# A delta-rule attention with two MLPs: stage b ahead of the merge in odd steps, one negation of 96 partitions, and GpSimd's zeros in place of two masks

## The chip, the cores and the metric

One core of a Trainium2 chip runs the whole program. The metric is device microseconds of one execution; the median of three runs of the kernel before is 896.2 us.

## The reference

The inputs are q, k, v of 4 batches x 8 heads x 768 tokens x 48 features and a step size beta. The attention is a recurrence over tokens, and its output feeds two dense blocks:

```python
for t in range(S):
    kt, vt, bt = (k_n[:, :, t], v[:, :, t], beta[:, :, t, None])
    y[:, :, t] = np.einsum('bhd,bhde->bhe', q[:, :, t], state)
    v_old = np.einsum('bhde,bhd->bhe', state, kt)
    state = state + bt[:, :, :, None] * np.einsum('bhd,bhe->bhde', kt, vt - v_old)
...
X = fft(fft(x, axis=1), axis=2); u = x + real(X)
y = u + relu(layernorm(u) @ w_ch1) @ w_ch2                      # 384 -> 1536 -> 384
h = relu(y @ w_in); u, v = halves(h)                            # 512 each
out = (u * (w_spatial @ layernorm(v) + b_spatial)) @ w_out
```

## The kernel before

**Chunks.** The recurrence is cut into 48 chunks of 64 tokens (12 of each batch, the batches interleaved), numbered bc. One chunk holds all 8 heads of its batch as 4 pairs, so a tile has 128 partitions: two heads of 64 tokens. Inside a chunk the recurrence is the inverse of a triangular 64x64 matrix. It is built from two 32x32 inverses and one corner block between them.

**The solve.** Six blocks of 8 chunks are inverted on VectorE (DVE). `prep` gathers the two 32x32 diagonal blocks of every head into `Cc`, masks them for blocks 1 and 2 only (L255), and transposes them into `Ts`. `root` reads their diagonal (`sq`, L140) and has ScalarE (ACT) take a square root (L141). `solve` runs the elimination column by column (L271 to L314) and transposes the inverse to `Tc` (L324). The solve of block j is spread over eight steps of the loop, and the `prep` and `root` of block j+1 stand at its end. GpSimd (POOL) only sets the diagonal to one (L274).

**The loop.** Step t, from -3 to 47, issues for different chunks:

- values (L400, ACT, four scalings of the loaded k and v of chunk t+2 by the norms);
- stage d of chunk t (L436 and L438 on TensorE, PE; then ACT copies the new state `Sb`, L449, and the output `x`, L453);
- stage c of chunk t+1 (L423 on PE, then `cw` on DVE, L424; stage d of that chunk multiplies by `cw`);
- stage a of chunk t+20 while there are such chunks (L217 on PE, then L223 on DVE);
- in odd steps `merge` of a pair of chunks, in even steps `diag` (L363, ACT);
- stage b of chunk t+2 (L407 on PE, then two ACT copies into `WU`, L412).

**The merge** makes the corner blocks of two chunks. PE interleaves two kinds of 32x32 matmuls into the one bank Z: `z0` (L375) for the pair that comes next, `z1` (L377) for the pair whose `z0` an earlier merge made. ACT then negates `z0` into `ZS` in two instructions of 32 partitions (L380), and copies `z1` into the inverse `TT` in two (L383). `z1` of the next merge reads `ZS`. Stage b of the pair reads `TT`, and first does so in the next, even step. At the first pair of a block an additional merge with `z0` alone stands between stage d and stage c (t % 8 == 5); at the last pair of a block the merge has `z1` alone.

**Order.** The engines execute what the code issues in the order of issue: `chain` ties every instruction to the one ahead of it on its engine. So the order in the code is the order in each engine's queue. From t = 37 on values and `diag` run on DVE, and pieces of the Fourier transform (L616 to L660) and of the weight conversion (L690 to L703) fill the gaps. The MLPs follow after about 300 us.

```python
qs = [slice(32 * u, 32 * u + 32) for u in range(4)]
lo, up = qs[::2], qs[1::2]
```

Of the kernel before, what the change touches and what calls it, by code (L numbers as in the profile page):

```python
# [7 lines left out]
F32 = mybir.dt.float32  # L8
# [12 lines left out]
C = 64  # L21
NC = S // C
HP = H // 2
NBC = B * NC
# [41 lines left out]
class Kernel:  # L66
# [51 lines left out]
    def attention(self, cp, pg, pe, p, x, filler, after_solves):  # L118
        nc, a, load = self.nc, self.a, self.load
        bt = cp.tile([128, NBC * HP], F32, name="bt")  # L120


        mk = cp.tile([128, 4 * C + 66], F32, name="mk")
        ZS = [cp.tile([128, 8, 64], F32, name=f"ZS{i}") for i in range(2)]
# [8 lines left out]
        gas, Tts, st, kqs, qts, preps, seen_a = {}, {}, {}, {}, {}, {}, [0]  # L133


        def root(blk):

            Tf, T = preps[blk]
            sq, n0 = (pe.tile([128, 32], F32, name=n, bufs=2) for n in ("sq", "n0"))
            nc.vector.tensor_copy(out=sq, in_=Tf[:, 0:1024:33])  # L140
            nc.scalar.sqrt(n0, sq)  # L141
            preps[blk] = Tf, T, sq, n0

# [100 lines left out]
        def prep(blk):  # L244


            Cc = pe.tile([128, 1024], F32, name="Cc").rearrange("p (g c) -> p g c", g=32)
            for h4 in range(2):
# [4 lines left out]
                yield 750  # L253
            if blk in (1, 2):
                nc.vector.tensor_mul(Cc, Cc, mk[:, 4 * C + 2 : 4 * C + 34].unsqueeze(1).to_broadcast([128, 32, 32]))  # L255
                yield 1200

            Tf = pe.tile([128, 1056], F32, name="Ts", bufs=CF["mb"])
            T = Tf[:, :1024].rearrange("p (i j) -> p i j", i=32)
            nc.vector.transpose(out=T, in_=Cc.rearrange("p g c -> p c g"))  # L260
            preps[blk] = Tf, T
            yield 2000
# [91 lines left out]
        lo, up = qs[::2], qs[1::2]  # L354
# [10 lines left out]
        def merge(g8, first, second):  # L365
# [4 lines left out]
            tt = TT[(g8 - 1) % NTT]  # L370
            for g in range(8):
                for h in range(2):
                    if first:
                        ga = gas[g8 * 2 + g // 4][:, g % 4]
                        nc.tensor.matmul(z0[up[h], g], lhsT=ga[up[h], C : C + 32], rhs=T0[up[h], o0 + g], start=True, stop=True)  # L375
                    if second:
                        nc.tensor.matmul(z1[lo[h], g], lhsT=T1[lo[h], o1 + g], rhs=ZS[(g8 - 1) % 2][lo[h], g], start=True, stop=True)  # L377
            if first:
                for h in range(2):
                    nc.scalar.mul(ZS[g8 % 2][lo[h], :, 32:], z0[up[h]], -1.0)  # L380
            if second:
                for h in range(2):
                    nc.scalar.copy(out=tt[lo[h], :, 64 * h : 64 * h + 64], in_=z1[lo[h]])  # L383

# [90 lines left out]
        for t in TT:  # L475
            nc.gpsimd.memset(t, 0.0)
        zz = self.bank("pz", [128, 512])
        for t in ZS:
            nc.scalar.copy(out=t[:, :, :32], in_=mk[:, 4 * C + 34 :].unsqueeze(1).to_broadcast([128, 8, 32]))
        for t in WU + Sb:  # L480
# [31 lines left out]
        T0 = -3  # L512
        for t in range(T0, NBC):
# [31 lines left out]
            if t < T0 + CF["kq"]:  # L545
                load_kq(HEAD + t - T0)
            if t % 2:
                g = (t + 3) // 2
                if g < NBC // 2:
                    merge(g + 1, (g + 1) % 4 > 0, True)  # L550
            elif t % 8 != 4 and t + 4 < NBC:
                diag((t + 4) // 2)
            if (t + 4) % 8 > 1 and t + 4 < NBC:
                load_kv(t + 4)
            if light(t):
# [4 lines left out]
                for _ in range(CF["cvt"][t - (NBC - 11)]):  # L560
                    next(tail, None)
            if 0 <= t + 2 < NBC:
                stage_b(t + 2)
# [544 lines left out]
def layout(q, k, v, beta, moe_w_ch1, moe_w_ch2, moe2_w_in, moe2_w_spatial, moe2_b_spatial, moe2_w_out):  # L1108
# [36 lines left out]
    j, s2 = KEY[s], np.where(s < 32, (s <= i) & (i < 32), (i < 32) | (s <= i))  # L1145
    o["mk"] = np.concatenate([j + i < C, s2, j < i, s2, s >= 32, s < 32, s % 32 <= i[:, :32], s % 32 == i[:, :32]], 1).astype(f)
    o["idn"] = np.eye(128, dtype=f)
# [69 lines left out]
```

## Time and profile before

| What | us |
| --- | --- |
| Median of 3 runs (lowest 895.42, highest 898.05) | 896.2 |
| The profiled execution | 895.05 |
| Its span in the profile, first to last instruction | 892.9 |
| PE busy over the span | 849.1 |
| DVE busy | 578.0 |
| ACT busy | 404.9 |
| POOL busy | 71.1 |
| Start to the first merge / loop with merges / MLPs | 0 to 41 / 41 to 275 / 300 to 893 |

An engine's busy time is the sum of its instructions' durations; neighbours on one engine overlap a little, so a sum can come close to the stretch without leaving a real gap. PE being busy 95% of the span says little of the loop: there its busy share changes from stretch to stretch, and what counts is which engine another waits for.

### The profile page before, as it was taken

To read this page: it belongs to the slowest core of one execution; us is meant where nothing else is said; L and a number is where in the kernel's file an instruction comes from. 1 tells how busy PE (TensorE), PEld (TensorE's weight loads), DVE (VectorE), ACT (ScalarE), POOL (GpSimd) and SP (SyncE) were. 2 spreads that over 40 slices of the span, in tenths; PEclk is the share of its full clock that TensorE was granted. 3 is DMA by queue.
4 is the path that set the end of the run, shared out by engine and by line. 5 is a ranking of instruction groups with operands and counts; after the bars stand their busy time and mean duration, and the time that the engine had idled before them with its cause. 6 is when DMAs were issued, how large, how long until landed. Compare 5 with 4: busy or idle time off the path is not lost.

```text
span 892.9 us, 18553 instructions
## 1 busy us (share of the span) xinstructions
PE 849.1 (95%) x7219; PEld 817.5 (92%) x7219; DVE 578.0 (65%) x1786; ACT 404.9 (45%) x1014; POOL 71.1 (8%) x75
## 2 busy tenths in 40 slices
PE   7779989998998899999999999999999999999998
PEld 7678989888898798999999999999889899899898
DVE  5999998988766898785574793431475562451622
ACT  2589888789875544321212352221262241341411
POOL 2000000000000000000000000000033232222221
PEclk8969999999999899999999999999999999999999
DMA  8264666633461710001022311101132210000001
GB/s 217 75 179 119 172 170 162 164 82 81 121 172 46 268 69 1 1 1 27 1 63 80 124 28 27 37 18 32 45 92 68 75 28 28 27 1 28 28 1 54
DMA packets 57674, 67.24 MB, mean 75 GB/s; under 512 B 31825, under 2 KB 48946, under 8 KB 57586
## 3 DMA queue, kind: packets, MB, share of 16 engines
q1 hardware_dynamic: 57586, 66.05, 26.0%
q8 instruction: 57, 0.93, 0.5%
q14 instruction: 31, 0.25, 0.1%
HBM read 53.64 MB, written 4.72 MB: 65 GB/s over the span
## 4 chain that ended last, share of the span: by engine, by line
PE 77%; DVE 12%; ACT 8%; issue 2%; DMA 1%; POOL 0%; ACTq 0%; DVEq 0%; POOLq 0%
PE bankX L801 15%; PE bankY L817 14%; PE bankX L940 11%; PE bankY L960 6%; PE bankX L926 5%; PE bankX L901 5%; PE bankY L423 4%; PE bankY L436 3%; PE bankY L438 2%; PE bankY L407 2%; PE bankX L217 2%; PE bankZ L377 2%; ACT WU L412 2%; ACT TT L383 2%; PE bankX L622 2%
## 5 line engine op out<-in xcount | busy, mean ns | idle before, releaser
L801 PE MATMUL bankX<-uh,w 128*128 128x384 f32 x504 | 136.8, 338 | 2.4 <-DVE ul L729 2.4
L817 PE MATMUL bankY<-w,hh 128*128 128x384 f32 x504 | 117.4, 339 | 1.1 <-DVE w L703 1.1
L808 ACT ACTIVATE hh<-bankX 128x384 fp32r<-128x384 f32 x84 | 41.2, 491 | 152.0 <-PE bankX L801 149.4
L809 DVE SCALAR_TENSOR_TENSOR hl<-bankX,hh 128x384 fp32r<-128x384 f32 x84 | 46.5, 554 | 97.5 <-ACT hh L808 97.4
L940 PE MATMUL bankX<-ws,vh 128*128 128x384 f32 x384 | 97.6, 336 | 0.0
L801 PEld LDWEIGHTS bankX<-uh,w 128*128 128x128 f32 x504 | 91.9, 188 | 3.1 <-DVE ul L729 2.9
L817 PEld LDWEIGHTS bankY<-w,hh 128*128 128x128 f32 x504 | 90.1, 188 | 2.2 <-DVE w L703 1.7
L801 PE MATMUL bankX<-ul,w 128*128 128x384 f32 x252 | 84.9, 337 | 0.0
L918 POOL TENSOR_TENSOR vl<-v,vh 128x512 fp32r<-128x512 f32 x24 | 31.8, 1335 | 519.8 <-DMA x<-un 442.7
L436 PE MATMUL bankY<-WU,gak 128*112 128x96 f32 (+1 forms) x384 | 69.0, 268 | 3.5 <-ACT x L453 3.2
L817 PE MATMUL bankY<-w,hl 128*128 128x384 f32 x252 | 72.2, 338 | 0.0
L940 PEld LDWEIGHTS bankX<-ws,vh 128*128 128x128 f32 x384 | 69.4, 188 | 0.0
L948 DVE TENSOR_TENSOR g<-bankX,bsb 128x384 f32<-128x384 f32 x32 | 17.7, 556 | 77.8 <-PE bankX L940 73.6
L438 PE MATMUL bankY<-Sb,cw 112*112 112x96 f32 (+1 forms) x352 | 63.9, 264 | 1.0 <-ACT w L702 0.7
L940 PE MATMUL bankX<-ws,vl 128*128 128x384 f32 x192 | 63.7, 336 | 0.0
L310 DVE TENSOR_TENSOR Ts<-Ts,tm 128x110 f32<-128x110 f32 (+26 forms) x264 | 60.4, 271 | 0.8
L305 DVE TENSOR_TENSOR tm<-Ts 128x110 f32<-128x110 f32 (+26 forms) x264 | 60.1, 270 | 0.4
L407 PE MATMUL bankY<-gak,TT 128*128 128x96 f32 x384 | 54.8, 288 | 5.1 <-issue 2.7
L436 PEld LDWEIGHTS bankY<-WU,gak 128*112 128x112 f32 (+1 forms) x384 | 52.7, 179 | 5.0 <-ACT x L453 4.8
L407 PEld LDWEIGHTS bankY<-gak,TT 128*128 128x128 f32 x384 | 49.1, 200 | 7.7 <-issue 3.0
L423 PE MATMUL bankY<-gak,WU 128*112 128x112 f32 x352 | 45.6, 274 | 8.0 <-ACT WU L412 8.0
L926 PE MATMUL bankX<-xh,s 128*128 128x384 f32 x192 | 50.3, 338 | 1.6 <-ACT v L910 1.6
(180 smaller groups left out, 1834.6 us busy)
## 6 DMA issues: line engine op xcount, KB each, us to landing
kq<-in_kq_dram SPq DMA_DIRECT2D x24, 448.0 KB, 4.3
qt<-in_qt_dram SPq DMA_DIRECT2D x48, 196.0 KB, 4.0
gak<-in_kv_dram SPq DMA_DIRECT2D x48, 192.0 KB, 4.0
w<-in_w_dram SPq DMA_DIRECT2D x24, 384.0 KB, 6.7
x<-un SPq DMA_DIRECT2D x128, 36.0 KB, 1.9
out_dram<-ot SPq DMA_DIRECT2D x24, 192.0 KB, 2.0
kq<-in_kc_dram SPq DMA_DIRECT2D x8, 448.0 KB, 11.5
s<-in_wi_dram SPq DMA_DIRECT2D x6, 512.0 KB, 4.8
```

What stands on the lines that cost most here:

```text
L305: nc.vector.tensor_tensor(out=tm, in0=T[:, r, k : k + 1].to_broadcast(sh), in1=T[:, k : k + 1, :k].to_broadcast(sh), op=MUL)
L310: nc.vector.tensor_add(o, o, tm)
L407: nc.tensor.matmul(pb[:, hp].rearrange("p t d -> p (t d)"), lhsT=tt[:, o + hp], rhs=kv[:, hp], start=True, stop=True)
L423: nc.tensor.matmul(pc[:, hp], lhsT=w[:, hp], rhs=gas[bc][:, hp, : C + D], start=True, stop=True)
L436: nc.tensor.matmul(pd[:m, hp], lhsT=ak[:, hp, :m], rhs=u[:, hp], start=True, stop=(c == 0))
L438: nc.tensor.matmul(pd[:m, hp], lhsT=cw[:, hp, :m], rhs=sb[:, hp], start=False, stop=True)
L801: nc.tensor.matmul(ph, lhsT=w1[f][i][:, c * 128 : c * 128 + 128], rhs=cur[k][:, c], start=(c + j == 0), stop=(c == 2 and j == 2))
L809: nc.vector.scalar_tensor_tensor(out=hl, in0=ph, scalar=0.0, in1=hh.bitcast(F32), op0=MAX, op1=SUB)
L817: nc.tensor.matmul(acc[t], lhsT=hx[i][:, t * 128 : t * 128 + 128], rhs=w2[e][k], start=(e == 0 and j == 0), stop=(e == 11 and j == 2),)
L926: nc.tensor.matmul(pu, lhsT=wi[2 * c][i][:, f * 128 : f * 128 + 128], rhs=xT[hf][k][:, c], start=(c + j == 0), stop=(c == 2 and j == 2),)
L940: nc.tensor.matmul(pv, lhsT=vn[i][:, s, f * 128 : f * 128 + 128], rhs=ws[2 * s + hf][k], start=(s + j == 0), stop=(s == 5 and j == 2),)
L960: nc.tensor.matmul(po, lhsT=gt[i][:, f, t * 128 : t * 128 + 128], rhs=wo[f][k], start=(f + j == 0), stop=(f == 3 and j == 2),)
```

## The change

Three edits, and what goes with them:

- **Order in odd steps.** Up to t = 43 stage b of chunk t+2 is issued ahead of the merge, no longer behind it. Even steps and the last two odd ones keep their order.
- **One negation.** `z0` is now written into the partitions 0 to 31 and 64 to 95 of bank Z, `z1` into 32 to 63 and 96 to 127 (they change places). One ACT instruction over the partitions 0 to 95 negates `z0`; it also negates the 32 partitions in between, which nobody reads. VectorE zeroes the bank once at the start. The copies into `TT` now go from one group of partitions to another.
- **Zeros in place of masks.** For blocks 1 and 2 the mask multiplication in `prep` is gone (and the step of 1200 that it counted for in the spreading of the solve). In its place `root` has POOL write zeros over the triangle of `Ts`, in five memsets of 256, 128, 64, 32 and 16 elements a partition. `Ts` is 16 columns wider, the table of masks 32 columns narrower.

```diff
-            Tf, T = preps[blk]
+            Tf, T, _ = preps[blk]
             sq, n0 = (pe.tile([128, 32], F32, name=n, bufs=2) for n in ("sq", "n0"))
             nc.vector.tensor_copy(out=sq, in_=Tf[:, 0:1024:33])
             nc.scalar.sqrt(n0, sq)
+            if blk in (1, 2):
+
+                for n in (16, 8, 4, 2, 1):
+                    t = preps[blk][2][:, n : n + 1056].rearrange("p (m q) -> p m q", q=66 * n)[:, :, : 32 * n]
+                    nc.gpsimd.memset(t.rearrange("p m (r w) -> p m r w", w=32)[:, :, :, :n], 0.0)
...
-            if blk in (1, 2):
-                nc.vector.tensor_mul(Cc, Cc, mk[:, 4 * C + 2 : 4 * C + 34].unsqueeze(1).to_broadcast([128, 32, 32]))
-                yield 1200
-
-            Tf = pe.tile([128, 1056], F32, name="Ts", bufs=CF["mb"])
+            Tw = pe.tile([128, 1072], F32, name="Ts", bufs=CF["mb"])
+            Tf = Tw[:, :1056]
...
-                        nc.tensor.matmul(z0[up[h], g], lhsT=ga[up[h], C : C + 32], rhs=T0[up[h], o0 + g], start=True, stop=True)
+                        nc.tensor.matmul(z0[lo[h], g], lhsT=ga[up[h], C : C + 32], rhs=T0[up[h], o0 + g], start=True, stop=True)
...
-                        nc.tensor.matmul(z1[lo[h], g], lhsT=T1[lo[h], o1 + g], rhs=ZS[(g8 - 1) % 2][lo[h], g], start=True, stop=True)
+                        nc.tensor.matmul(z1[up[h], g], lhsT=T1[lo[h], o1 + g], rhs=ZS[(g8 - 1) % 2][lo[h], g], start=True, stop=True)
             if first:
-                for h in range(2):
-                    nc.scalar.mul(ZS[g8 % 2][lo[h], :, 32:], z0[up[h]], -1.0)
+                nc.scalar.mul(ZS[g8 % 2][:96, :, 32:], z0[:96], -1.0)
             if second:
                 for h in range(2):
-                    nc.scalar.copy(out=tt[lo[h], :, 64 * h : 64 * h + 64], in_=z1[lo[h]])
+                    nc.scalar.copy(out=tt[lo[h], :, 64 * h : 64 * h + 64], in_=z1[up[h]])
...
         zz = self.bank("pz", [128, 512])
+        nc.vector.memset(zz, 0.0)
...
-            if t % 2:
+            odd = t % 2 and (t + 3) // 2 < NBC // 2
+            if odd and 0 <= t + 2:
+                stage_b(t + 2)
+            if odd:
                 g = (t + 3) // 2
-                if g < NBC // 2:
-                    merge(g + 1, (g + 1) % 4 > 0, True)
-            elif t % 8 != 4 and t + 4 < NBC:
+                merge(g + 1, (g + 1) % 4 > 0, True)
+            if t % 2 == 0 and t % 8 != 4 and t + 4 < NBC:
                 diag((t + 4) // 2)
...
-            if 0 <= t + 2 < NBC:
+            if not odd and 0 <= t + 2 < NBC:
                 stage_b(t + 2)
```

How the edits move instructions shows best in three places of the queues. The first is PE's queue in the odd step t = 19, at the last pair of a block, where the merge has only its 16 matmuls of `z1` (L377). Before, in the order stage c, stage a, merge, stage b, and stage d of the next step:

```order
L423 MATMUL bankY<-gak,WU_87 112x112 x4
L217 MATMUL bankX<-kq 128x128 x4
L377 MATMUL bankZ<-ZS_81,Tc 32x64 x16
L407 MATMUL bankY<-gak,TT_85 128x96 x4
L436 MATMUL bankY<-WU_87,gak 112x96
L438 MATMUL bankY<-Sb_91,cw 112x96
```

And now, with the changed kernel's line numbers (stage b is L408, the merge L379, stage d L437 and L439):

```order
L424 MATMUL bankY<-gak,WU_87 112x112 x4
L222 MATMUL bankX<-kq 128x128 x4
L408 MATMUL bankY<-gak,TT_85 128x96 x4
L379 MATMUL bankZ<-ZS_81,Tc 32x64 x16
L437 MATMUL bankY<-WU_87,gak 112x96
L439 MATMUL bankY<-Sb_91,cw 112x96
```

Stage b and the merge have changed places; all else stands where it stood.

The second place is ACT's queue in the odd step t = 13, the first pair of a block with its two merges. Before, with both negations in two halves (L380), the copies of the inverse (L363, L383), the copies of stage b (L412), and the scalings of the next step (L400):

```order
L380 ACTIVATE ZS_80<-bankZ 32x8x32 x2
L363 COPY TT_85<-Tc 32x8x32 x2
L380 ACTIVATE ZS_81<-bankZ 32x8x32 x2
L383 COPY TT_85<-bankZ 32x8x64 x2
L412 COPY WU_88<-bankY 64x4x2x48 x2
L400 ACTIVATE gak<-gak,n_all 128x48 x4
```

And now (negation L381, copies L365 and L384, copies of stage b L413, scalings L401):

```order
L381 ACTIVATE ZS_80<-bankZ 96x8x32
L365 COPY TT_85<-Tc 32x8x32 x2
L413 COPY WU_88<-bankY 64x4x2x48 x2
L381 ACTIVATE ZS_81<-bankZ 96x8x32
L384 COPY TT_85<-bankZ 32x8x64 x2
L401 ACTIVATE gak<-gak,n_all 128x48 x4
```

The two `WU` copies now come ahead of the odd merge's negation and `TT` copies, and each negation is one instruction.

The third place is DVE's queue at the end of the solve of block 1, where block 2 is prepared. Before (L250 gathers, L255 is the mask, L424 a step's `cw`, L260 and L324 transposes, L237 and L223 masks of stage a, L140 the diagonal):

```order
L250 SCALAR_TENSOR_TENSOR Cc<-gak,mk 128x512 x2
L255 TENSOR_TENSOR Cc<-Cc,mk 128x1024
L424 TENSOR_TENSOR cw<-qt,bankY 112x448
L260 STREAM_TRANSPOSE Ts<-Cc 128x1024
L237 TENSOR_TENSOR gak<-gak,mk 128x8x64
L324 STREAM_TRANSPOSE Tc<-Ts 128x16x32
L223 TENSOR_TENSOR gak<-bankX,mk 128x4x128
L140 COPY sq<-Ts 128x32
L324 STREAM_TRANSPOSE Tc<-Ts 128x16x32
```

And now (L255 gathers, L262 and L326 transposes, L425 is `cw`, L242 and L228 are the masks of stage a):

```order
L255 SCALAR_TENSOR_TENSOR Cc<-gak,mk 128x512 x2
L262 STREAM_TRANSPOSE Ts<-Cc 128x1024
L425 TENSOR_TENSOR cw<-qt,bankY 112x448
L242 TENSOR_TENSOR gak<-gak,mk 128x8x64
L326 STREAM_TRANSPOSE Tc<-Ts 128x16x32
L140 COPY sq<-Ts 128x32
L326 STREAM_TRANSPOSE Tc<-Ts 128x16x32
L228 TENSOR_TENSOR gak<-bankX,mk 128x4x128
```

The multiplication is gone, and the transposes and the diagonal stand one of the loop's instructions earlier than before. The first elimination instruction of blocks 1 and 2 (L271 before, L273 now) gains a wait for POOL.

## Rows read from the trace of the kernel before

**Rows 1.** Windows: stretch, us, busy PE, PEld, DVE, ACT, POOL, clock, DMA share, GB/s.

```profile
0.00:8.00 8.00, 6.23 (x46) 6.11 (x48) 0.00 (x0) 1.69 (x3) 5.27 (x13) 1.00 0.77 205
40.60:81.60 41.00, 31.36 (x476) 29.35 (x477) 40.19 (x152) 32.13 (x91) 0.15 (x1) 0.79 0.54 142
81.60:123.10 41.50, 39.81 (x578) 37.95 (x577) 39.18 (x154) 34.81 (x98) 0.17 (x2) 1.00 0.61 168
123.10:165.60 42.50, 39.19 (x574) 37.19 (x573) 38.78 (x150) 35.25 (x98) 0.15 (x1) 1.00 0.60 163
165.60:205.30 39.70, 36.51 (x546) 34.91 (x546) 35.64 (x143) 34.03 (x97) 0.19 (x2) 1.00 0.41 105
205.30:242.50 37.20, 34.67 (x535) 31.86 (x528) 28.05 (x82) 34.20 (x93) 0.12 (x1) 1.00 0.36 95
```

**Rows 2.** Chain that ended last, 135 to 143 us: start, us, what.

```profile
135.51 0.38 ACT ZS L380
...
136.29 0.57 ACT TT L383
...
137.48 0.48 ACT WU L412
...
138.50 1.04 PE bankY L423 x8
...
140.44 0.87 PE bankY L407 x8
...
142.89 0.80 PE bankY L423 x8
```

**Rows 3.** Waits, 81.6 to 123.1 us: us in total, times, longest us.

```profile
DVE cw L424 <- PE bankY L423: 1.8, 2, 1.2
...
PE bankY L423 <- ACT WU L412: 0.8, 2, 0.4
```

**Rows 4.** Waits, 123.1 to 205.3 us.

```profile
DVE cw L424 <- PE bankY L423: 5.7, 6, 2.1
...
PE bankY L423 <- ACT WU L412: 4.2, 6, 1.2
...
ACT n L141 <- DVE sq L140: 2.4, 2, 1.5
```

**Rows 5.** Waits of PE, 205.3 to 242.5 us.

```profile
PE bankY L423 <- ACT WU L412: 1.6, 4, 0.5
```

**Rows 6.** Waits of PE, 242.5 to 300 us.

```profile
PE bankY L423 <- ACT WU L412: 1.1, 3, 0.5
```

**Rows 7.** Groups by line and form, DVE's L255: busy us, mean ns.

```profile
L255 DVE TENSOR_TENSOR Cc<-Cc,mk 128x1024 f32<-128x1024 f32 x2 | 2.4, 1224 | 0.1
```

**Rows 8.** Chain that ended last, 45 to 48 us.

```profile
45.75 0.20 DVE sq L140
...
47.29 1.04 DVE Ts L271 x2
```

**Rows 9.** Groups by line and form, POOL's memsets: busy us, mean ns, idle before.

```profile
L481 POOL MEMSET Sb<- 112x384 f32 x4 | 1.5, 418 | 0.0
L274 POOL MEMSET Ts<- 128x32 f32 x6 | 0.9, 156 | 198.7 <-DVE Ts L271 198.7
```

**Rows 10.** Groups by line and form, ACT, 0 to 300 us.

```profile
L380 ACT ACTIVATE ZS<-bankZ 32x256 f32<-32x256 f32 x48 | 18.1, 376 | 13.3 <-PE bankZ L377 12.7
...
L221 ACT COPY gak<-bankX 128x256 f32<-128x256 f32 x16 | 6.2, 387 | 0.0
```

**Rows 11.** Timeline of PE, 134.25 to 134.36 us: start, us, engine, line.

```profile
134.30 0.21 PE L375 MATMUL bankZ<-Tc,gak 32*32 32x32 f32 x1
134.31 0.24 PE L377 MATMUL bankZ<-ZS,Tc 32*32 32x64 f32 x1
```

More of the change, by code (lines that the diff above doesn't have):

```diff
@@ L120, in attention @@
         bt = cp.tile([128, NBC * HP], F32, name="bt")
-        mk = cp.tile([128, 4 * C + 66], F32, name="mk")
+        mk = cp.tile([128, 4 * C + 34], F32, name="mk")
         ZS = [cp.tile([128, 8, 64], F32, name=f"ZS{i}") for i in range(2)]
@@ L253, in prep @@
                 yield 750
-            if blk in (1, 2):
-                nc.vector.tensor_mul(Cc, Cc, mk[:, 4 * C + 2 : 4 * C + 34].unsqueeze(1).to_broadcast([128, 32, 32]))
-                yield 1200
-            Tf = pe.tile([128, 1056], F32, name="Ts", bufs=CF["mb"])
+            Tw = pe.tile([128, 1072], F32, name="Ts", bufs=CF["mb"])
+            Tf = Tw[:, :1056]
             T = Tf[:, :1024].rearrange("p (i j) -> p i j", i=32)
             nc.vector.transpose(out=T, in_=Cc.rearrange("p g c -> p c g"))
-            preps[blk] = Tf, T
+            preps[blk] = Tf, T, Tw
             yield 2000
@@ L477, in attention @@
         zz = self.bank("pz", [128, 512])
+        nc.vector.memset(zz, 0.0)
         for t in ZS:
-            nc.scalar.copy(out=t[:, :, :32], in_=mk[:, 4 * C + 34 :].unsqueeze(1).to_broadcast([128, 8, 32]))
+            nc.scalar.copy(out=t[:, :, :32], in_=mk[:, 4 * C + 2 :].unsqueeze(1).to_broadcast([128, 8, 32]))
         for t in WU + Sb:
@@ L1145, in layout @@
     j, s2 = KEY[s], np.where(s < 32, (s <= i) & (i < 32), (i < 32) | (s <= i))
-    o["mk"] = np.concatenate([j + i < C, s2, j < i, s2, s >= 32, s < 32, s % 32 <= i[:, :32], s % 32 == i[:, :32]], 1).astype(f)
+    o["mk"] = np.concatenate([j + i < C, s2, j < i, s2, s >= 32, s < 32, s % 32 == i[:, :32]], 1).astype(f)
     o["idn"] = np.eye(128, dtype=f)
```

## The prediction

> **What bounds the kernel now.** The MLPs, from 300 us on, keep TensorE (PE) full, and the change doesn't touch them. So I read the loop, by stretches that are about one block of eight steps each: first the windows, for which engine has no room left; then the chain, for what the time goes through; then the waits, for what PE and DVE lose.
>
> The windows [rows 1] show two different bounds. From 40.6 to 81.6 us (block 1) DVE is busy 40.19 of 41.00 us: it is the bound there. In blocks 2 to 4 PE (39.8 of 41.5, 39.2 of 42.5, 36.5 of 39.7) and DVE (39.2, 38.8, 35.6) are both nearly full, and either can hold the other. From 205.3 to 242.5, without stage a, DVE has room (28.1 of 37.2), and PE (34.7) and ACT (34.2) are close to full.
>
> The chain through an odd step [rows 2] shows why PE isn't quite full: the merge ends, ACT negates in two halves from 135.51 (0.38 us each), copies twice into `TT` (0.57 us each), and only then makes the two `WU` copies of stage b (0.48 each). PE, done with stage b and stage d by then, takes up stage c at 138.50. There stage c takes 1.04 us, against 0.80 where it follows on without a gap, at 142.89. I call the 0.24 us between them the restart.
>
> The waits say how often. PE waits at stage c for `WU` 0.8 us in block 2 (2 times), 4.2 in blocks 3 and 4 (6), 1.6 from 205.3 to 242.5 (4) and 1.1 after that (3) [rows 3 to 6]. DVE waits for PE at `cw` 1.8 us in block 2 and 5.7 in blocks 3 and 4 [rows 3, 4]. That is nearly all the slack that DVE has there.
>
> **The order of stage b and merge.** PE does the same matmuls as before. ACT's `WU` copies no longer stand behind the merge: they start when stage b ends, and their 2 x 0.48 us run beside the merge (from 134.30 [rows 11] to about when ACT can negate, 135.51 [rows 2], 1.2 us). Their reader, stage c, stands behind the merge and stage d. Stage d is 142.89 - (140.44 + 0.87) = 1.58 us [rows 2], so the cover is 2.8 us for 1.0 us of work: the wait goes away. What is late next is `TT`. Its copies end 0.38 + 2 x 0.57 = 1.5 us, plus a handover of 0.1, after the merge. The first reader is stage b of the next step, behind stage d (1.58) and stage c (0.80): 2.4 us where there is no stage a, about 0.9 more where there is. So it is hidden with 0.8 us to spare; a merge longer by more than that would show. Queued on ACT behind the negation's wait for the merge are the `TT` copies, the scalings of the next step and the copies of the state, as before; only the two `WU` copies have left that queue. No DMA moves past another on SP. In the step with two merges stage b's 0.87 us now lies between them, during which ACT negates: PE's wait for the first negation goes too.
>
> **One negation.** It removes 24 of the 48 instructions of 0.376 us: 9.0 us of ACT over the loop. For 96 partitions there is no row; a copy of the same 256 columns on 128 partitions takes 0.387 us, on 32 partitions 0.376 [rows 10]. Between these ends I take 0.38. It is worth its 0.376 us where ACT sets the pace, and nothing where its work is hidden. Its wait now covers `z1` too, but that is interleaved with `z0`, so it ends at the same time.
>
> **Zeros for masks.** DVE loses two multiplications of 1.224 us [rows 7], both in the stretch where DVE is full: 2.45 us. Four of POOL's memsets lie between sizes that the trace has: 0.156 us for 32 columns, 0.418 for 384 [rows 9]; the fifth is smaller still. On that line 256, 128, 64, 32 and 16 columns come to 0.32 + 0.23 + 0.18 + 0.16 + 0.14 = 1.0 us; at 0.156 each it would be 0.8, at 0.418 each 2.1. They can start when the diagonal has been read, at 45.95, and the elimination starts at 47.29 [rows 8], 1.34 us later. So they hide if the line holds; at the upper end 0.8 us of the first 1.22 is given back once. In block 2 the second transpose to `Tc` lies between as well. The zeroing of the bank is one DVE instruction in a stretch in which DVE does nothing at all (0.00 of 8.00 [rows 1]); half the width of the 1.224 us row, it costs at most 0.6 us, and hides. The narrower mask table spares 16 KB of a load; I count nothing.
>
> **The sum.** Block 1: DVE full, so what leaves DVE leaves the time: -2.45 (ends: -1.2, if POOL is late or PE can't follow, and -3.3, with DVE's last 0.8 us of room).
>
> Blocks 2 to 4: PE could gain its waits and restarts: in block 2 0.8 + 2 x 0.24 = 1.3, in blocks 3 and 4 4.2 + 6 x 0.24 = 5.6; together 6.9. DVE must follow, and can by its idle time: 1.8 and 5.7. That is no less in either part, but 5.6 of 5.7 would have DVE run for 82 us almost without a gap. I leave 0.9 of it and take 1.3 + 4.7 = 6.0 (ends: 2 and 6.9).
>
> 205.3 to 242.5: PE could gain 1.6 + 4 x 0.24 = 2.6, but ACT has to follow. It sheds five negations there, 1.9 us; with part of its 3.0 us of idle time, 2.2 (ends: 1.5 and 2.6).
>
> 242.5 to 300: 1.1 + 3 x 0.24 = 1.8. Against it: at the last merge (t = 43) the ACT copies of the Fourier transform now queue behind two `WU` copies, 0.96 us, and the end of the loop hangs on them. I take 1.0 (ends: 0 and 1.8).
>
> Together 2.45 + 6.0 + 2.2 + 1.0 = 11.65 us. The profiled execution took 895.05 us, so 883.4 for its like. It lies 1.15 us below the median of the runs, 896.2, so I expect a median of **884.5 us**.
>
> **The rivals.**
>
> *DVE takes the gain back.* In blocks 2 to 4 the solve and its root end when DVE ends, and ACT stands still for them: 2.4 us before the two square roots of blocks 3 and 4 [rows 4]. If PE's lead only lengthens the waits for `cw` and for the root, blocks 2 to 4 give 1 to 3 us in place of 6.0. For it: DVE busy 39.2 of 41.5 and 38.8 of 42.5 us. Against it: its listed waits for PE are as long as the gain that I want from them. Time: 896.2 - (2.45 + 2 + 2.2 + 1.0) = 888.5; with the low ends elsewhere too, 891.
>
> *All of PE's waits go, and more.* The upper ends: 3.3 + 6.9 + 2.6 + 1.8 = 14.6 us, 881.6; with another 1 us from the waits between the merges, 880.6. Against it: DVE would have to lose every gap.
>
> *The reordering does nothing.* If ACT's work in even steps were so tight that the waits only move to stage d or b, the masks alone would remain, and some of the negations: 2.45 + 1.5, so 892. Against it: in blocks 2 to 4 ACT is busy 34 to 35 of 40 to 42 us.
>
> *Slower: the merge's matmuls no longer overlap.* `z0` now goes from rows 32 to 63 of the array to the columns 0 to 31, `z1` from rows 0 to 31 to the columns 32 to 63: the paths cross, which no row before shows. If the 32 matmuls of a merge took turns, at 0.21 to 0.24 us each [rows 11], a merge would take 7 us in place of 1.2. Eighteen merges have both kinds: about +100 us, 985. It decides from 11.65 / 18 = 0.65 us more per merge on. Against it: `z0` and `z1` already use different rows and columns, and start 0.01 us apart [rows 11].
>
> A rule would have it so. The Trainium skill, "TensorEngine Tiling (Array Packing)", section Restrictions and Gotchas, says that different row tiles cannot access the same PSUM bank at the same time. By that rule the merge of before would take turns too, since `z0` and `z1` share bank Z; the trace disagrees, with starts at 134.30 and 134.31 us, so I keep the rule at a small chance.
>
> **How the numbers follow.** Chances: the sum as forecast, a gain of 9 to 14 us, 0.62; DVE takes part of it back (gain 5 to 9), 0.18; all waits go and more (over 14), 0.08; the masks alone and little else (2.7 to 5), 0.04, or under 2.7, 0.04; slower by the merge or another queue, 0.04. The range from 880 to 891 takes in the first three but for their tails, 0.85. About 0.3%, 2.7 us, is what a measurement of this kernel can tell from no change: faster by more than that 0.62 + 0.18 + 0.08 + 0.04 = 0.92, of which I take 0.02 off for what I haven't thought of; so 0.90, the same 0.05, slower 0.05.
>
> **What would show it.** Right, in the profile of the changed kernel: the waits of stage c for `WU` are nearly gone; the negations are 24 of about 0.38 us; a merge's matmuls still start a few hundredths of a us apart; DVE's waits for `cw` in blocks 2 to 4 shrink from 7.5 us to 1 or 2; the first elimination instruction of block 1 starts 1.2 us earlier and doesn't wait for POOL; and the loop's events at 81.6, 205 and 300 us come about 2.4, 8.5 and 11.7 us earlier. Wrong: new waits of stage d for `cw` that add up to several us, longer waits of ACT before the square root, waits of stage b for `TT`, a merge of over 1.8 us, or memsets that hold up the elimination.

## The result, and the profile after

The changed kernel takes 888.63 us and the kernel before 895.83 on the same chip; the ratio of the two is 0.9917, with a 95% interval of 0.9895 to 0.9938. The 888.63 is the median of three executions; a fourth was disturbed and took 2917.63 us, and with it the median would be 888.95. So the change gains 7.2 us. The forecast was a gain of 11.65, of which six tenths came; the time lies inside the range, near its upper end. The profiled execution has a span of 886.5 us against 892.9.

To see where the 6.4 us of span went, I read the start of five events in PE's timeline: the first matmul of a merge at the start of block 1, of block 2, behind block 4 and at t = 37, and the 43rd stage c, which the end of the loop follows. Before (start, us, engine, line):

```profile
40.70 0.22 PE L375 MATMUL bankZ<-Tc,gak 32*32 32x32 f32 x2 [1.55 <-DVE Tc L324]
...
79.65 0.22 PE L375 MATMUL bankZ<-Tc,gak 32*32 32x32 f32 x2 [0.76 <-DVE w L148]
...
204.82 0.22 PE L375 MATMUL bankZ<-Tc,gak 32*32 32x32 f32 x2
...
241.85 0.22 PE L375 MATMUL bankZ<-Tc,gak 32*32 32x32 f32 x2
...
284.92 0.28 PE L423 MATMUL bankY<-gak,WU 128*112 128x112 f32 x1
```

And after:

```profile
40.86 0.22 PE L377 MATMUL bankZ<-Tc,gak 32*32 32x32 f32 x2 [1.85 <-DVE Tc L326]
...
78.76 0.22 PE L377 MATMUL bankZ<-Tc,gak 32*32 32x32 f32 x2
...
198.81 0.22 PE L377 MATMUL bankZ<-Tc,gak 32*32 32x32 f32 x2
...
234.38 0.25 PE L377 MATMUL bankZ<-Tc,gak 32*32 32x32 f32 x4
...
278.51 0.28 PE L424 MATMUL bankY<-gak,WU 128*112 128x112 f32 x1
```

The differences between neighbours say how much each stretch gained. Block 1 took 37.90 us for 38.95: -1.05 (forecast -2.45). Blocks 2 to 4 gave -5.12 (forecast -6.0), 205 to 242 us -1.46 (-2.2), and the last stretch, which was to give -1.0, lost 1.06. Behind it, 608.0 us to the end of the span as before.

The windows of the stretches that answer to block 1 and to two of the next three in [rows 1], in the same columns:

```profile
39.70:80.70 41.00, 31.83 (x476) 29.58 (x477) 39.42 (x151) 30.15 (x86) 1.65 (x12) 0.79 0.55 142
80.70:121.00 40.30, 39.28 (x578) 37.85 (x577) 39.09 (x154) 34.20 (x95) 0.15 (x1) 1.00 0.64 172
121.00:161.50 40.50, 39.08 (x574) 37.31 (x572) 38.36 (x150) 34.07 (x94) 0.08 (x1) 1.00 0.64 172
```

The same matmuls of blocks 2 and 3 lie in stretches that are 1.2 and 2.0 us shorter, and PE's gaps there are down to 1.0 and 1.4 us, from 1.7 and 3.3. In block 1 DVE has 1.6 us of room where it had 0.8.

The waits answer to [rows 3, 4]. Those of PE from 80.7 to 199 us (us in total, times, longest us) are one group:

```profile
PE bankY L437 <- ACT x L454: 4.0, 5, 1.2
```

Those of all engines from 121 to 199.3 us:

```profile
ACT WU L413 <- PE bankY L408: 6.0, 7, 1.2
...
DVE cw L425 <- PE bankY L424: 3.0, 3, 1.4
...
PE bankY L437 <- ACT x L454: 2.9, 4, 1.2
...
ACT n L141 <- DVE sq L140: 2.6, 2, 1.6
```

The waits of stage c for `WU` (5.0 us, 8 times) have no row any more. Now ACT waits for stage b, which means that the `WU` copies begin when stage b ends. What has grown is stage d's wait for the copies of the state (`x`): 4.0 us, 5 times. ACT's wait for the root's diagonal is about as long as it was (2.6 us for 2.4). Before, stage d's wait in the same blocks (81.6 to 205 us) was:

```profile
PE bankY L436 <- ACT x L453: 2.8, 3, 1.1
```

One odd step, to be held against [rows 2]: ACT's timeline of the merge at 132.03 us (start, us).

```profile
132.13 0.97 ACT L413 COPY WU<-bankY 64x384 f32<-64x384 f32 x2 [0.85 <-PE bankY L408]
133.18 0.38 ACT L381 ACTIVATE ZS<-bankZ 96x256 f32<-96x256 f32 x1
133.57 1.17 ACT L384 COPY TT<-bankZ 32x512 f32<-32x512 f32 x2
```

The `WU` copies end at 133.10, and stage c, which needs them, starts at 134.70, right behind stage d. The cover is there, as worked out. The negation's group (busy us, mean ns, idle before):

```profile
L381 ACT ACTIVATE ZS<-bankZ 96x256 f32<-96x256 f32 x24 | 9.1, 378 | 3.3 <-PE bankZ L379 2.2
```

And POOL's timeline at the five memsets of block 1:

```profile
44.90 0.67 POOL L146 MEMSET Ts<- 128x256 f32 x5 [26.21 <-DVE sq L140]
```

Both parts cost what they were taken for, or less: 378 ns (0.38), and 0.67 us for the five memsets (1.0). They end at 45.57, ahead of the elimination at 46.34.

### The profile page after: what moved, and what is told of

Read it like the earlier page. It is cut to its first block, busy times and chain, and to the rows that moved or that the text cites. A ratio compares the mean times of both kernels' runs of the same rounds, so it can differ in the third digit from the quotient of the medians.

```text
span 886.5 us, 18540 instructions
## 1 busy us (share of the span) xinstructions
PE 848.0 (96%) x7219; PEld 817.9 (92%) x7219; DVE 575.9 (65%) x1785; ACT 397.2 (45%) x990; POOL 72.5 (8%) x85
## 4 chain that ended last, share of the span: by engine, by line
PE 80%; DVE 11%; ACT 5%; issue 2%; DMA 1%; POOL 0%; ACTq 0%; DVEq 0%; POOLq 0%
PE bankX L805 15%; PE bankY L821 14%; PE bankX L944 11%; PE bankY L964 6%; PE bankX L930 5%; PE bankX L905 5%; PE bankY L408 4%; PE bankY L437 4%; PE bankY L424 3%; PE bankY L439 3%; PE bankX L222 2%; PE bankZ L379 2%; PE bankX L626 2%; PE bankV L821 1%; PE bankX L642 1%
## 5 line engine op out<-in xcount | busy, mean ns | idle before, releaser
L437 PE MATMUL bankY<-WU,gak 128*112 128x96 f32 (+1 forms) x384 | 70.8, 273 | 5.9 <-ACT x L454 5.8
L439 PE MATMUL bankY<-Sb,cw 112*112 112x96 f32 (+1 forms) x352 | 64.2, 265 | 1.0 <-ACT w L706 0.8
L437 PEld LDWEIGHTS bankY<-WU,gak 128*112 128x112 f32 (+1 forms) x384 | 52.6, 179 | 10.0 <-ACT x L454 7.7
L408 PE MATMUL bankY<-gak,TT 128*128 128x96 f32 x384 | 52.9, 283 | 9.2 <-ACT gak L401 3.5
L408 PEld LDWEIGHTS bankY<-gak,TT 128*128 128x128 f32 x384 | 49.1, 200 | 10.3 <-issue 4.2
L413 ACT COPY WU<-bankY 64x384 f32<-64x384 f32 x96 | 45.4, 473 | 19.6 <-PE bankY L408 17.9
```

The costliest lines, as they stand in the source:

```text
L408: nc.tensor.matmul(pb[:, hp].rearrange("p t d -> p (t d)"), lhsT=tt[:, o + hp], rhs=kv[:, hp], start=True, stop=True)
L413: nc.scalar.copy(out=o_, in_=pb[hs])
L437: nc.tensor.matmul(pd[:m, hp], lhsT=ak[:, hp, :m], rhs=u[:, hp], start=True, stop=(c == 0))
L439: nc.tensor.matmul(pd[:m, hp], lhsT=cw[:, hp, :m], rhs=sb[:, hp], start=False, stop=True)
```

## The experiments

All ran against the kernel before on one chip per batch (medians 896.15, 895.95 and 895.8 us). The theory: the prediction's accounting by stretches holds, and what is missing was lost at single places (the first steps, where stage b now waits for its values ahead of the merge; the last stretch). The rival: DVE takes the gain back in blocks 2 to 4. The first four kernels take the edits apart. The next four undo the order, restore DVE's order and relieve DVE. The last four narrow the stretch of the order and repeat the changed kernel.

### The parts alone

**The order alone.** Against the kernel before:

```diff
+            odd = t % 2 and (t + 3) // 2 < NBC // 2
+            if odd and 0 <= t + 2:
+                stage_b(t + 2)
...
-            if 0 <= t + 2 < NBC:
+            if not odd and 0 <= t + 2 < NBC:
```

> The kernel before with the new order of stage b and merge alone (two negations, both masks stay). Theory A (each edit takes away a wait where its engine sets the pace, and the new order costs where stage b's values come late): blocks 2 to 4 gain about 5 us as in the changed kernel, 205 to 242 us about 1, the head nothing (DVE keeps its masks), the last stretch loses about 1 to 2 (stage b waits for values on DVE at t = 39, 41 and 45): 890.5 to 892, 4 to 5.5 us less than before. Rival B (DVE is the bound in blocks 2 to 4 and only the lighter DVE let PE gain): 894 to 896.

895.92 us, ratio 0.9996 (0.9987 to 1.0005): by the medians nothing, which is the time that rival B gave. But B's reason fell too, since DVE kept its masks and blocks 2 to 4 still gain 3.85 us in the trace. 205 to 242 us gives 0.66, block 1 loses 1.6 and the last stretch 1.04: the loop is 1.87 us shorter, in an execution that is the shortest of the twelve (893.57 us, against 895.12 for the shortest of the kernel before). So the edit that was to carry most of the gain carries little by itself.

The 1.6 us of block 1 can't be put down to the order alone, which costs 0.3 to 0.5 there beside the masks. In this execution the granted clock was at 0.50 (1.2 GHz) until about 63.2 us, in the kernel before until about 59.2, and in between DVE waited 1.4 us for a stage c. The windows from 60 to 62 us (busy PE, PEld, DVE, ACT, POOL, clock), before and with the order alone:

```profile
60.00:62.00 2.00, 1.74 (x16) 1.61 (x16) 2.00 (x11) 1.88 (x6) 0.00 (x0) 1.00 0.00 0
...
60.00:62.00 2.00, 2.00 (x13) 2.00 (x13) 0.91 (x5) 1.96 (x6) 0.00 (x0) 0.50 0.25 65
```

How much of the 1.6 us is the clock's stays open.

**The masks alone,** that is POOL's zeros in place of the two masks. Against the kernel before:

```diff
-            if blk in (1, 2):
-                nc.vector.tensor_mul(Cc, Cc, mk[:, 4 * C + 2 : 4 * C + 34].unsqueeze(1).to_broadcast([128, 32, 32]))
-                yield 1200
...
+                    nc.gpsimd.memset(t.rearrange("p m (r w) -> p m r w", w=32)[:, :, :, :n], 0.0)
```

> The kernel before with POOL's zeros for the two masks alone. Theory A: DVE gains 2.4 us in block 1, of which PE takes the 0.8 us that it waited at the first merge of block 2 and part of the earlier start of the first merges; after that PE's waits for WU are as before, so DVE's lead is idle time: 1 to 2.4 us less than before, 893.5 to 895. Rival B (DVE is the bound through blocks 1 to 4): the whole 2.4 us and more idle time of DVE nowhere, 893 to 893.5.

895.79 us, ratio 0.9994 (0.9985 to 1.0003). Block 1 is 1.36 us shorter, and blocks 2 to 4 give 0.78 of it back; why was not followed up. Both theories miss (893 to 895).

**The negation alone,** with the exchanged partitions and the zeroed bank that it needs. Against the kernel before:

```diff
...
-                for h in range(2):
-                    nc.scalar.mul(ZS[g8 % 2][lo[h], :, 32:], z0[up[h]], -1.0)
+                nc.scalar.mul(ZS[g8 % 2][:96, :, 32:], z0[:96], -1.0)
...
```

> The kernel before with the one negation of 96 partitions alone (with the exchanged partitions and the zeroed bank). Theory A: in the order of before the negation stands ahead of the copies into TT and WU, so each of the 11 odd merges with both kinds after which stage c waited for WU ends 0.38 us earlier, and the two additional ones at the first pair too: 3 to 4.5 us less than before, 891.5 to 893; this edit and the new order would then pay for the same waits twice, which the sum of the prediction left out. Rival (the negation counts only from 205 to 242 us, as the sum had it): 1.5 to 2 us less. Rival (crossed paths slow the merge): slower than before.

889.75 us, ratio 0.9933 (0.9921 to 0.9944): nearly all of the gain, and more than expected. ACT's timeline in the same odd step:

```profile
133.89 0.38 ACT L379 ACTIVATE ZS<-bankZ 96x256 f32<-96x256 f32 x1 [1.33 <-PE bankZ L377]
134.28 1.17 ACT L382 COPY TT<-bankZ 32x512 f32<-32x512 f32 x2
135.48 0.97 ACT L411 COPY WU<-bankY 64x384 f32<-64x384 f32 x2
```

What is left of PE's waits in blocks 2 to 4 (79.8 to 201.3 us):

```profile
PE bankY L435 <- ACT x L452: 2.8, 3, 1.1
PE bankY L422 <- ACT WU L411: 1.7, 2, 0.8
```

The `WU` copies still stand behind the negation, and one negation less brings them 0.38 us forward. Of the eight waits of 5.0 us six are gone, and the two long ones are 0.4 shorter: 3.3 us of waits, and the stretch is 3.65 shorter.

**All edits, the order for 1 <= t < 37 alone.** Against the changed kernel:

```diff
-            if odd and 0 <= t + 2:
+            ahead = odd and 1 <= t < 37
+            if ahead:
...
-            if not odd and 0 <= t + 2 < NBC:
+            if not ahead and 0 <= t + 2 < NBC:
```

> The changed kernel with stage b ahead of the merge only from t = 1 to 35; at t = -1 and from t = 37 on in the old order. Theory A (in the changed kernel stage b then waits for its values: 1.5 us at t = -1, 0.9 us each at t = 39 and 41, and the Fourier copies behind the WU copies cost 1.2 us at t = 45): 2.5 to 4 us less than the changed kernel, 885 to 886.5. Rival B (those waits only take the place of others, for DVE or ACT): within 1 us of the changed kernel, 888 to 890.

887.89 us, ratio 0.9913 (0.9901 to 0.9925), between the two theories, and nearer to B. In the trace the last stretch gains 1.26 where the changed kernel loses 1.06; so that loss is the order's.

### The order undone, DVE's order restored, DVE relieved

**Masks and negation, the old order.** Against the changed kernel:

```diff
-            if odd and 0 <= t + 2:
-                stage_b(t + 2)
...
-            if not odd and 0 <= t + 2 < NBC:
+            if 0 <= t + 2 < NBC:
```

> Negation and masks, with stage b left behind the merge: the changed kernel with its new order undone. Theory A (the negation and the new order pay for the same waits of stage c; alone in blocks 2 to 4 they gave 3.65 and 3.85 us, together 5.1, and the order loses about 2 us behind 242 us): 888.5 to 890 us, within 1 us of the changed kernel, and the loop's last stage d 6.3 to 7 us earlier than before. Rival B (the new order carries a part of the gain that the negation doesn't): 890.5 to 892. Rival C (the order costs more than it gives once the negation is there): 887 to 888.5.

888.58 us, ratio 0.9913 (0.9897 to 0.9929), where theories A and C meet: the changed kernel without the new order is as fast as with it, or a little faster. The trace speaks for C. The last stage c comes 7.30 us earlier than before, where A had at most 7, and from the start of block 1 to there the loop is 1.1 us shorter than that of the changed kernel. It is also 1.28 us shorter than with the negation alone, by what block 1 gives (1.34 for 0.01): beside the negation the masks are worth that much.

**The solver's step kept,** on top of the order for 1 <= t < 37.

```diff
+            if blk == 2:
+                yield 1200
             Tw = pe.tile([128, 1072], F32, name="Ts", bufs=CF["mb"])
```

> All three edits, the new order only for 1 <= t < 37, and the solver's step of 1200 that stood behind the mask of block 2 is kept, so that cw of t = 4 stands ahead of the 1.97 us transpose again. Theory A (the second mask's 1.22 us is lost because the transpose took its place in front of that cw): cw starts near 72 us in place of 73.8, the wait of stage d for it (0.66) goes, stage a of that step starts at 75.2 to 75.4 in place of 75.94, and 0.6 to 0.7 us of that stay to the end: about 887.2. Rival B (PE's path through block 1 doesn't hang on that cw): stage a at 75.9 and 887.9 as without the step.

Without the mask the transpose of block 2 came to stand ahead of a step's `cw`. DVE's timeline in the changed kernel:

```profile
72.12 1.96 DVE L262 STREAM_TRANSPOSE Ts<-Cc 128x1024 f32<-128x1024 f32 x1
74.02 0.57 DVE L425 TENSOR_TENSOR cw<-qt,bankY 112x448 f32<-112x448 f32 x1
```

And with the step kept:

```profile
72.81 0.62 DVE L427 TENSOR_TENSOR cw<-qt,bankY 112x448 f32<-112x448 f32 x1
73.34 1.95 DVE L264 STREAM_TRANSPOSE Ts<-Cc 128x1024 f32<-128x1024 f32 x1
```

Before, `cw` started at 73.89: the second mask left DVE, and the `cw` that PE waits for came no earlier. With the step kept it does, and block 1 is 1.91 us shorter in place of 1.36. But blocks 2 to 4 give 4.51 in place of 5.01, since the solve of block 2 now starts behind that `cw`, and stage d waits for DVE once (PE's waits, 79 to 100 us):

```profile
PE bankY L441 <- DVE cw L427: 0.6, 1, 0.6
```

So the wait went where theory A had it, and its 0.6 us came back one block later; that half of theory A fell. The median, 886.93 us (ratio 0.9896, 0.9881 to 0.9911), is the lowest of all kernels that compute everything, but from the start of block 1 (41.96 us there, 41.02 without the step) to the last stage c its loop is only 0.2 us shorter than without the step.

**DVE relieved.** From the changed kernel, and from the kernel before, DVE's masking of q.k is left out for the chunks from 8 on, so those products stay unmasked.

```diff
-            if t % 2 == 0 and 2 <= t + 2 < HEAD:
+            if t % 2 == 0 and 2 <= t + 2 < 8:
```

> The changed kernel without DVE's masking of q.k for the chunks from 8 on (the products stay unmasked), which takes some 3 us of DVE's work out of each of blocks 2 and 3. Theory A (behind block 1, PE's and ACT's chain sets the pace and DVE only the root): 888.3 to 889 us, and the three waits of stage d for the state at the ends of the blocks (1.02, 1.03, 1.23) stay above 0.8. Rival B (DVE takes the gain back in blocks 2 to 4): 886 to 887.5 and those waits shrink by 0.5 or more.

> The kernel before with the same masking left out. Theory A (PE waits for ACT there, not for DVE): 895.5 to 896.5, the waits of stage c for WU as before. Rival B (DVE is a bound in blocks 2 to 4 already): 893.5 to 895.

Medians 889.64 (ratio 0.9927, 0.9906 to 0.9948) and 895.2 us (0.9997, 0.9984 to 1.001): the first lies above both theories (its four executions take 888.14 to 891.23), the second between its two. The traces say more. Blocks 2 to 4 are 6.92 us shorter than before in place of 5.12, and without the change 1.31 shorter. The waits for the state (PE, 79.6 to 197.8 us) are shorter:

```profile
PE bankY L437 <- ACT x L454: 2.6, 5, 1.2
```

Two of the three long ones, at the ends of blocks 2 and 3, fall from 1.0 to 0.35. The whole times show little of it: both profiled executions began block 1 later (41.57 and 42.27 us), the changed kernel keeps its loss in the last stretch, and that of the kernel before lost 3.1 us behind the loop (see the last section). So rival B is right for a part: DVE's root holds PE up by 0.7 us a block at two blocks, before as after, and of the change's own gain DVE keeps 1.8 - 1.3 = 0.5 us.

### Where the order pays

**The order up to t = 35, from its first step.** Against the kernel with the order for 1 <= t < 37:

```diff
-            ahead = odd and 1 <= t < 37
+            ahead = odd and -2 <= t < 37
```

> All three edits, the new order from its first step (t = -1) up to t = 35: only the last stretch goes back to stage b behind the merge. Theory A (the order loses its gain behind 242 us, where stage b then waits for values that DVE makes behind the pieces of the Fourier transform, and the first steps cost nothing that lasts, since DVE is full there): the last stage c of the loop 8.4 to 8.7 us earlier than before, as with the order for t = 1 to 36; 887 to 888. Rival B (the wait of stage b for its values at t = -1 costs about 1 us that lasts): 7.3 to 7.7 us earlier, 888.3 to 889.

887.41 us, ratio 0.9903 (0.9889 to 0.9918). The last stretch gains 1.29. Its stage c ends up 7.60 us earlier, but block 1 began 1.16 later than before, so 8.76 from there: theory A for the stretch that was put back. The first steps did cost half of what rival B said: block 1 is 0.89 us shorter, and 1.36 to 1.38 with the old order at t = -1.

**The order in blocks 2 to 4 alone.** Against the same kernel:

```diff
-            ahead = odd and 1 <= t < 37
+            ahead = odd and 5 <= t < 29
```

> All three edits, the new order only in blocks 2 to 4 (5 <= t < 29). Theory A (the order adds to the negation only there, 1.4 to 1.6 us, since from 205 to 242 us the two pay for the same waits): the last stage c 8.4 to 8.9 us earlier than before, 887 to 888. Rival B (the order adds nothing that the slower last stretch doesn't take): 7.2 to 7.5 us earlier as with negation and masks, 888.3 to 889.

887.41 us, ratio 0.9903 (0.9887 to 0.9918); its last stage c is 8.61 us earlier. Blocks 2 to 4 give 5.12 as in the changed kernel and 205 to 242 us 1.54 without the order, so theory A.

**The same with DVE relieved,** those products unmasked.

> The same, and without DVE's masking of q.k for the chunks from 8 on (those products stay unmasked): some 3 us less for DVE in each of blocks 2 and 3. Theory A (the two roots at the ends of blocks 2 and 3 hold up stage d by 0.7 us each, and DVE's work beside it by 0.4 more): blocks 2 to 4 give 1.4 to 1.9 us more than with the masking, 885.3 to 886.5. Rival B (ACT's and PE's chain alone sets the pace): within 0.4 of the run with the masking.

885.81 us, ratio 0.9886 (0.987 to 0.9902); blocks 2 to 4 give 6.89, which is 1.77 more: theory A.

**The changed kernel again.**

> The changed kernel once more, on the same chip as three of its variants, for a narrower interval than its first four executions gave. Theory A (the new order is worth nothing beside the negation): 888.5 to 889.5, 0.5 to 1.5 us behind the kernel that has the order in blocks 2 to 4 alone. Rival B (the order is worth what its gain in blocks 2 to 4 says): 887 to 888 and level with it.

889.52 us, ratio 0.9925 (0.9911 to 0.9939), 2.1 us behind the order in blocks 2 to 4 alone: theory A's side, and by more than it said. The two intervals of the ratio overlap a little, but the loops of the two are 2.9 us apart in the table below (-9.33 and -6.39).

### All stretches together

What each stretch gained (-) or lost against the kernel before, by the same five events in PE's timeline; the first column is the shift of the first event, which differs between two executions of one kernel too.

| Kernel | start | block 1 | blocks 2 to 4 | 205 to 242 | last |
| --- | --- | --- | --- | --- | --- |
| changed | +0.16 | -1.05 | -5.12 | -1.46 | +1.06 |
| changed, again | +0.98 | -0.89 | -5.10 | -1.45 | +1.05 |
| order alone | +0.29 | +1.60 | -3.85 | -0.66 | +1.04 |
| masks alone | +0.30 | -1.36 | +0.78 | +0.08 | +0.01 |
| negation alone | +0.14 | -0.01 | -3.65 | -1.47 | -1.28 |
| masks, negation | +0.39 | -1.34 | -3.50 | -1.56 | -1.29 |
| all, order 1 to 36 | +0.32 | -1.36 | -5.01 | -1.35 | -1.26 |
| the same, step kept | +1.26 | -1.91 | -4.51 | -1.45 | -1.31 |
| all, order to 35 | +1.16 | -0.89 | -5.12 | -1.46 | -1.29 |
| all, order 5 to 28 | +0.72 | -1.38 | -5.12 | -1.54 | -1.29 |
| the same, DVE relieved | +1.17 | -1.35 | -6.89 | -1.53 | -1.30 |
| changed, DVE relieved | +0.87 | -0.89 | -6.92 | -1.45 | +1.04 |
| before, DVE relieved | +1.57 | +0.17 | -1.31 | -0.03 | -0.01 |

Two kernels with the same code in a stretch agree there within 0.2 us, far closer than the medians, whose intervals are 1.6 to 4 us wide. The table's use is to read down a column. The new order is worth 5.12 - 3.50 = 1.6 us in blocks 2 to 4 beside the negation, which is the size of the two waits for `WU` (1.7 us) that the negation leaves there. It is worth nothing from 205 to 242 us, and it costs 0.3 to 0.5 in block 1 and 1.06 + 1.29 = 2.35 in the last stretch. The four columns behind the start add up to -6.57 for the changed kernel and to -7.69 for masks and negation: over the loop the new order costs 1.1 us.

Block 1 is the one stretch that runs in part at the lower clock. The clock rose some 16 us behind the first event with the order for 5 <= t < 29 and with the step kept (57.3 and 58.4 us), and some 19 us behind it with masks and negation (60.0 us). The first and the last of these gain the same (1.38 and 1.34), so the 1.91 with the step kept isn't the clock's. With the order alone it rose some 22 us behind.

## Why the prediction was right, and where its sizes were off

**The sign and the mechanism were right.** Stage c's waits for `WU` were the slack of blocks 2 to 4, ACT's queue behind the merge was their cause, and they are gone. The time came out nearer than the terms: the gain lies in the bracket of 5 to 9 us, which had a chance of 0.18 and stood for DVE taking part of it back, and not in that of 9 to 14 with its 0.62. Over the loop 5.1 us of the forecast are missing: 1.4 in block 1, 0.9 in blocks 2 to 4, 0.7 from 205 to 242 us and 2.1 in the last stretch. So the loop's events come 0.9, 6.0 and 6.4 us earlier and not 2.4, 8.5 and 11.7. The negations are 24 of 0.378 us, the memsets hide, and the first elimination of block 1 starts 0.95 us earlier and waits for no one (it was to be 1.2).

**The attribution was wrong.** The prediction gave blocks 2 to 4 wholly to the order and called a negation worth its 0.376 us where ACT sets the pace, and nothing where its work is hidden, and it counted negations from 205 to 242 us alone. But [rows 2] show both halves on the chain in front of the `WU` copies, in the steps in which stage c waits. So the negation alone takes 3.65 us there, the order alone 3.85, and both 5.12: two edits that pay for the same waits. *The reordering does nothing* is what the medians show of the order alone, but not for its reason: in blocks 2 to 4 the waits did go. Its loop is 1.9 us shorter by the one trace, and beside negation and masks the order makes the loop 1.1 us longer, since what it gains in blocks 2 to 4 it loses in the first and last steps.

**Block 1: -1.05 for -2.45.** "DVE full, so what leaves DVE leaves the time" holds for DVE: it reads the diagonal of block 2 at 76.11, 2.33 us earlier than before (78.44). It doesn't hold for PE. The first mask came through (1.36 with the old order, for its 1.22). The second stood ahead of the `cw` at t = 4, and with the mask the step of 1200 went, so that a 1.96 us transpose took its place and `cw` started at 74.02 for 73.89. With the step kept block 1 gives 1.91. The order printed ahead of the prediction showed the transposes moved; that `cw` was the row to follow there, I didn't see. Besides, the order costs 0.3 to 0.5 us in the first steps, where stage b, now ahead of the merge, waits for its values. PE in the changed kernel at the two places (the brackets are the idle time ahead of the row, and what ended it):

```profile
49.41 2.02 PE L408 MATMUL bankY<-gak,TT 128*128 128x96 f32 x8 [2.05 <-ACT gak L401]
52.89 2.02 PE L408 MATMUL bankY<-gak,TT 128*128 128x96 f32 x8 [1.46 <-ACT gak L401]
```

The second of them, at t = -1, is new.

**Blocks 2 to 4: -5.12 for -6.0.** A mis-sized term with the right bounds. The prediction left 0.9 us of PE's 6.9 (waits and restarts) to DVE. With DVE relieved 6.92 and 6.89 came, but that this meets the 6.9 is chance: the kernel before gains 1.31 of it as well, in two waits for the root that the 6.9 didn't count. PE's own part of the gain is 5.6, and DVE keeps 0.5 of that. The other 1.3 are not taken apart; two new waits of stage d for the state, 0.33 and 0.35 us, stand among them. *DVE takes the gain back* said 1 to 3 us for these blocks: too low, but its place, the root, was right. That its 888.5 us nearly came is chance too, since most of what is missing lies elsewhere. DVE's waits for `cw` fell from 7.5 to 4.1 us (1.1 up to 121 us and 3.0 behind it), not to 1 or 2.

**205 to 242 us: -1.46 for -2.2.** PE's waits for `WU` went from 1.6 us to 0.3, and new ones of stage d for the state took 1.4 (3 times). The negation alone gives the same.

**The last stretch: +1.06 for -1.0.** The step that failed: the prediction asked of stage b only when `TT` is ready, and put its other input at nothing. Stage b also reads the scaled values, which DVE makes from t = 37 on. PE's three new waits (timeline; the steps t = 39, 41 and 44), and DVE ahead of the first:

```profile
244.65 1.10 PE L408 MATMUL bankY<-gak,TT 128*128 128x96 f32 x8 [0.91 <-PE bankY L424]
254.40 1.10 PE L408 MATMUL bankY<-gak,TT 128*128 128x96 f32 x8 [0.91 <-ACT x L454]
276.00 1.10 PE L408 MATMUL bankY<-gak,TT 128*128 128x96 f32 x8 [1.20 <-DVE gak L398]
```

```profile
243.86 0.25 DVE L600 TENSOR_TENSOR s<-s 128x95 f32<-128x95 f32 x1
244.03 0.25 DVE L601 TENSOR_TENSOR s<-s 128x95 f32<-128x95 f32 x1
244.20 0.35 DVE L398 TENSOR_TENSOR gak<-gak,n_all 128x192 f32<-128x192 f32 x1
```

The values (L398) stand behind pieces of the Fourier transform (L600, L601) and end at 244.55; stage b starts at 244.65. The brackets of the first two rows name engines that were done earlier (the copy of `x` at 254.17, for one): the values are the last of what stage b waits for, at 254.40 as well (they end at 254.29). With the merge ahead of stage b this was hidden under the merge's 1.0 us. With the old order PE's waits in this stretch have one row, 0.2 us for `WU` (235.8 to 280 us, masks and negation). Up to stage c of t = 43 (266.29 us) these two waits cost 1.54 us against the order in blocks 2 to 4 alone, which has the old order here.

The third wait stands in t = 44, whose own order is as before. Here came what the prediction did set against this stretch. At t = 43 the Fourier pieces now stand behind stage b, and the values of the next step behind them. PE's first of these pieces starts 2.79 us after stage c of t = 43 and not 1.91 (timeline: changed; order in blocks 2 to 4 alone, where stage c starts at 264.90):

```profile
269.08 2.92 PE L642 MATMUL bankX<-s,s 96*128 96x96 f32 x24
...
266.81 2.92 PE L643 MATMUL bankX<-s,s 96*128 96x96 f32 x24
```

From stage c of t = 43 to that of t = 45 this costs 0.81 us, near the 0.96 of the prediction. With the 1.54 it makes the 2.35 of the table.

**The rivals of a slower kernel.** The crossed paths don't cost anything: in the changed kernel a merge's two kinds of matmul start together (PE's timeline).

```profile
132.03 0.21 PE L377 MATMUL bankZ<-Tc,gak 32*32 32x32 f32 x1
132.03 0.24 PE L379 MATMUL bankZ<-ZS,Tc 32*32 32x64 f32 x1
```

The Trainium skill, "TensorEngine Tiling (Array Packing)", section Restrictions and Gotchas, says that different row tiles cannot access one PSUM bank simultaneously. Both kinds write bank Z from different rows, at 132.03 us each, and the merge takes 1.0 us as before; in this kernel the rule costs no time. The price of this rival was too low: the trace has 64 rows for such a merge and not 32, so taking turns would have cost twice the 7 us. And the low ends of *DVE takes the gain back* add up to 891.5 and not 891.

**A version that beats both** leaves stage b behind the merge outside blocks 2 to 4: 887.41 us with the order for 5 <= t < 29, 1.2 to 2.1 us ahead of the changed kernel by medians. Its loop is the shortest of all that compute everything (-9.33 over the four columns).

## What to carry to other kernels

Where a wait hangs on an engine's queue, every microsecond in that queue ahead of the late instruction has the same price, whichever instruction it belongs to, and the cheapest edit (one negation of 0.38 us) can take most of what a reordering promises; price each edit alone, then together. An instruction that is moved forward needs all of its inputs earlier: list every tile that it reads, and who makes each in each stretch of the loop, since that may change from one stretch to the next. List also what it now stands ahead of. Work that leaves a full engine helps another engine only where the row that the other waits for moves as well.

## What was not expected of the hardware

Two profiled executions of the same changed kernel begin block 1 at 40.86 and 41.68 us, and then run the loop within 0.2 us of each other in every stretch: of the 1.1 us between their spans (886.5 and 887.6) 0.82 are made ahead of block 1.

In the profiled execution of the order for 1 <= t < 37 the granted clock fell inside the MLPs. PE had stood still for 1.85 us until 642.17; the windows (stretch, us, busy times, then the clock behind POOL's) show its lower level, 1.2 GHz, from behind 643 until nearly 647:

```profile
642.00:643.00 1.00, 0.83 (x5) 0.83 (x6) 0.82 (x2) 0.38 (x2) 1.00 (x1) 1.00 0.81 263
643.00:644.00 1.00, 1.00 (x6) 1.00 (x5) 0.77 (x4) 1.00 (x3) 0.04 (x1) 0.75 0.70 206
644.00:646.00 2.00, 2.00 (x7) 2.00 (x7) 1.97 (x8) 1.15 (x4) 0.00 (x0) 0.50 0.29 67
646.00:647.00 1.00, 1.00 (x5) 1.00 (x5) 0.15 (x1) 0.00 (x0) 0.00 (x0) 0.54 0.72 207
```

It took 609.7 us from its 43rd stage c to the end where the changed kernel takes 608.0. The same wait of 1.66 us in the run with the order in blocks 2 to 4 left the clock at 1.00.

The profiled execution of the kernel before with DVE relieved took 898.18 us, 3.0 more than its median, and 611.1 from its 43rd stage c to the end. PE waits 2.67 us there, ahead of stage b at 288.94, as it does ahead of 288.55 in the kernel before. In the kernel before the clock fell during that wait. Here it stayed at 1.00, and fell behind a second wait, of 1.94 us ahead of a stage c at 293.56. The windows at the lower level, before and in this execution:

```profile
288.00:294.70 6.70, 6.15 (x32) 6.18 (x33) 6.08 (x21) 2.92 (x8) 0.00 (x0) 0.50 0.28 67
...
294.70:304.80 10.10, 7.81 (x34) 6.61 (x32) 7.62 (x18) 3.69 (x8) 0.00 (x0) 0.50 0.47 148
```

The same matmul behind it (L786) starts 21.95 us after the 43rd stage c in the kernel before (306.87) and 24.52 after it here (309.83), so 2.6 of the 3.1 us are lost there. In this execution the place of the fall made most of the longer time. Whether that holds for the other longer executions (889.85 against 886.73 us for the order for 1 <= t < 37) stays open.

Each of POOL's memsets in the changed kernel was about as long as the line through two sizes said (312 ns for 256 columns, where it gave 0.32 us; 126 ns for 16, where it gave 0.14). But they overlap: the five take 0.67 us from the first to the last.
